# Layer 2 of the last pair of tiles split around its output projection; the last tile cut at column 288

## The chip, the cores and the metric

The kernel runs on one core of one Trainium2 chip, with the engines PE (TensorE, matrix multiply), DVE (VectorE), ACT (ScalarE), POOL (GpSimd) and SP (SyncE), which wait for each other through semaphores. The metric is device time in microseconds (us) of one execution, as the median of the runs; a lower one is better.

## The reference

One input x (2048 rows of 448 features, bf16) is normalised once, and the sum of x, a linear attention A and a dense layer B is returned:

```python
xn = _layernorm(x)
# A: 16 heads of 28
q, k, v = split(xn @ wqkv)
phi(q) = [softmax(q @ w_phi), softmax(-q @ w_phi)]      # the same for k: 56 features a head
kv = einsum("bhsf,bhsd->bhfd", phi_k, v);  z = sum_s phi_k
o  = (phi_q @ kv) / (phi_q @ z + 1e-6)
A  = o.reshape(B, S, D) @ wo
# B: 448 -> 1792 -> 448
h  = silu(xn @ w1)                                       # layer 1
out = h @ w2                                             # layer 2
return x + A + B
```

## The kernel before

The 2048 rows are 16 tiles of 128 rows; two neighbouring tiles are a pair, so tiles 14 and 15 are pair 7. For each tile a PSUM bank (128 x 448, f32) collects layer 2 of B (14 slices of 128 hidden features, `hT` times `w2_sb`) and the output projection of A (`oT_sb` times `wo_sb` and `wor_sb`). Then one addition on DVE (`out_ev`, lines 998 to 1004; the profile names its line 1000) adds x or an earlier partial sum and writes the result into `x_sb`, and a DMA stores it.

Most matmuls contract over only 64 rows. TensorE is then used as two halves, rows 0 to 63 (LOW) and rows 64 to 127 (HIGH), and `rows64` (lines 902 to 925) places matmuls of the two tiles of a pair alternately on the two halves, so that a LOW one and a HIGH one run at a time. I call such a pair of simultaneous matmuls a step. A block comes in two turns: in turn "a" the first tile has the LOW half, in turn "b" the second. When a bank changes its half, `rows64` sets `o.after` to the last block that used it, and TensorE waits on its own semaphore (s_pe) for that block's end.

The order of TensorE's work is written out by hand as the string `PLAN` (lines 361 to 368), and `strict` (line 1077) chains it; DVE, ACT, POOL and the SP queue are ordered by a list scheduler (`P.schedule`, line 228) that estimates durations. The words that matter here:

- `aG7` / `bG7`: 7 of the 14 slices of layer 2 for pair 7 on the two halves, `ffn2_pair` (line 932); `@672` gives the banks, 6 for tile 14 and 7 and 2 for tile 15.
- `aW7` / `bW7`: the output projection of pair 7, `wo_pair` (line 983): 4 steps in turn a, 3 in turn b. It needs `oT_sb`, the attention's output, transposed by a DMA on the SP queue (`oT_dma`, line 981, issued in `dma_t`, line 624). In the profile `oT_sb` is part of the tile `vaug`.
- `bW1`: the second turn of pair 1's projection, 3 steps; it belongs to other tiles.
- `E14` / `E15`: layer 2 of one tile with all 128 rows as one array, `ffn2_full` (line 940), followed by that tile's `out_ev`.

Tile 15 has two banks, so that its columns are finished in two pieces (`halves`, line 927, cut at column 224): the first piece is added and stored while TensorE computes the second. The store of a piece goes out on the ACT queue, that of the last piece on the SP queue. The last words of `PLAN` before the change are `bW6 bW7@672 bW1 aW7 E14 E15`. Tiles before pair 7 do not change.

Of the kernel before, what the change touches and what calls it, by code (L numbers as in the profile page):

```python
# [364 lines left out]
K6 K4 aq4@2 K12 aq8@4 bq4 K8 K2 s4 aq0@0 bq8 aq6@2 K14 bq0 bq6 bY1@45 K10 M aY1 aq2@2 aF26@0 s6 bq2 bY1 bF26 aG3@23 aY1  # L365
aU2@67 s8 aF15@0 bU2 s0 bF15 aF16@4 bG3 bF16 aU4@01 aq12@6 bU4 bq12 aU3@45 bG3 bU3 s2 aG3 aq10@0 aq14@6 bq10 s10 aW2@45
bq14 aG2 aU0@01 bG2 aG4@67 bU0 bW4 bG2 bW2 s12 bG4 aG2 s14 aW3 aG4 aU1@01 bW3 aW4 bU1 bG4 bG5@23 aU5@50 aG6@41 aU6@67
bU5 aG5 bG6 aU7@05 bU6 bG5 bG6 aG5 bU7 aG6 aW0@67 bW5 bW0 aW5 aW6 aW1@05 bW6 bW7@672 bW1 aW7 E14 E15"""


def bass_parallel_sum__linear_kernel_hedgehog__dense_activation_silu__prompt_kernel(
# [10 lines left out]
    S, D, H, DH, FF = 2048, 448, 16, 28, 1792  # L382
# [3 lines left out]
    FT = FF // 128  # L386
# [21 lines left out]
    with es:  # L408
        def sb(name, shape, dt):
            return es.enter_context(nc.sbuf_tensor(name, shape, dt))  # L410
# [25 lines left out]
        w2_sb = sb("w2_sb", [128, FT, D], BF16)  # L436
        hT = sb("hT", [128, FT, S], BF16)
# [54 lines left out]
        banks = [psum[:, i * 512:(i + 1) * 512] for i in range(8)]  # L492
# [10 lines left out]
        def d_mm(n):  # L503
            return max(n * 0.4167 + 2.5, 40.0)
# [10 lines left out]
        def pe_mms(mms, name, dur=None, keys_w=(), mode=128):  # L515
            def fn(e):
                r = None
                for dst, lhsT, rhs, st, sp in mms:
                    r = e.matmul(dst, lhsT, rhs, start=st, stop=sp, skip_group_check=True)  # L519
                return r  # L520
            n = 1
            for _, cnt in mms[0][2].ap[1:]:
                n *= cnt
            o = P.op("pe", dur if dur is not None else d_mm(n), fn, reads=[m[1] for m in mms] + [m[2] for m in mms],
                     writes=[m[0] for m in mms], keys_w=keys_w, name=name, mode=mode)
            o.words = 2 * len(mms)
            return o
# [20 lines left out]
        def memset(dst, v, n, name, eng="pool"):  # L548
            P.op(eng, d_pool(n, 0.5), lambda e: e.memset(dst, v), writes=[dst], name=name)
# [289 lines left out]
        def ones_column(t0, t1):  # L839
            dst = ek_pairs(t0, t1)[:, :, 0:2 * EW].rearrange("p i (h f) -> p i h f", f=DH)[:, :, :, DF]  # L840
            memset(dst, 1.0, 290 * (t1 - t0), f"one{t0}")
# [55 lines left out]
        def opens(bs):  # L897
            fresh.update(bs)
            for b in bs:
                half_of.pop(b, None)  # L900
# [25 lines left out]

        def halves(t, bs):

            cuts = (0, D) if len(bs) == 1 else (0, D // 2, D)
            return [(b, slice(0, c1 - c0), slice(c0, c1)) for b, c0, c1 in zip(bs, cuts, cuts[1:])]  # L930

        def ffn2_pair(p, turned, bs, f0, f1, last):
            both = []
            for side in range(2):
                i = side ^ turned
                both.append([(b, ds, hT[LO_HI[side], ft, (2 * p + i) * 128:(2 * p + i + 1) * 128], w2_sb[LO_HI[side], ft, cs])
                             for ft in range(f0, f1) for b, ds, cs in halves(2 * p + i, bs[i])])
            rows64(*both, "ffn2_mm", (f1 - f0) * d_mm(D), 0.0, last)

        def ffn2_full(t, bs):  # L940
            for b, ds, cs in halves(t, bs):
                pe_mms([(banks[b][:, ds], hT[:, ft, t * 128:(t + 1) * 128], w2_sb[:, ft, cs], False, ft == FT - 1) for ft in range(FT)],
                       "ffn2_mm", dur=FT * d_mm(cs.stop - cs.start))
                out_ev(t, banks[b][:, ds], x_sb[:, t, :], cs)

        def y_ev(t, b):
            fb = banks[b][:, 0:D]
            P.op("dve", d_dve(448), lambda e: e.tensor_tensor(Y_sb[:, t, :], fb, x_sb[:, t, :], ALU.add),  # L948
                 reads=[fb, x_sb[:, t, :]], writes=[Y_sb[:, t, :]], name="y_ev")
# [5 lines left out]
        def att(p, turned, bs):  # L955
            both = []
            for side in range(2):
                i = side ^ turned
                both.append([(bs[i], slice(c * 2 * DA, (c + 1) * 2 * DA), ph_slots(slot(2 * p + i))[LO_HI[side], 0, c, :],
                              KVm[LO_HI[side], c, :, :].rearrange("p j e -> p (j e)")) for c in range(CC)])  # L960
            rows64(*both, "U_mm", CC * 31.2, 400.0, turned)
            if turned:
                for i in range(2):
                    normalise(2 * p + i, banks[bs[i]])
# [33 lines left out]
        def out_ev(t, ob, addend, cs):  # L998
            res = x_sb[:, t, :]
            P.op("dve", d_dve(cs.stop - cs.start), lambda e: e.tensor_tensor(res[:, cs], ob, addend[:, cs], ALU.add),  # L1000
                 reads=[ob, addend[:, cs]], writes=[res[:, cs]], name="out_ev")
            P.dma(lambda e: e.dma_start(out=rows_of(out, t, t + 1)[:, 0, cs], in_=res[:, cs]), 100.0, lat=1200.0, reads=[res[:, cs]], name="out_dma", out_slot=ob_cnt[0] % NOS,
                  eng="sp" if cs.start else "act")
            ob_cnt[0] += 1
# [4 lines left out]
        def finish_pair(p, bs):  # L1009
            for i in range(2):  # L1010
                out_ev(2 * p + i, banks[bs[i][0]][:, 0:D], addend(2 * p + i), slice(0, D))
# [26 lines left out]
        for word in "tr0a tr0 tr1 00a 10a 01a 11a 00b 10b 01b 11b tr2 20 21 tr3 02 12 22 03 13 23".split():  # L1038
# [3 lines left out]
            f, t = int(word[0]), int(word[1])  # L1042
# [41 lines left out]
        blocks, bank_of, done = {}, {}, {}  # L1084
        open_kind = {"F": F, "v": v_block, "k": k_block, "q": q_block}

        def pair_banks(p, at):
            if at:
                b = [int(c) for c in at]
                bank_of[p] = (b[:1], b[1:])  # L1090
                opens(b)
            return bank_of[p]

        for word in PLAN.split():
            n0 = len(P.ops)
            kind, arg = word[0], word[1:]
            if kind == "r":
                b, f = (0, 2, AUX)[int(arg)], head[int(arg)]
                pe_mms(f[1](), "rest", dur=d_mm(512), mode=64)
                f[3]()  # L1100
            elif kind in "ab":
                turned = kind == "b"
                kind, (arg, _, at) = arg[0], arg[1:].partition("@")
                t = int(arg)
                if kind in open_kind:
                    if turned:
                        blocks[kind, t][2](1)
                        blocks[kind, t][3]()
                    else:
                        blocks[kind, t] = open_kind[kind](t, int(at))  # L1110
                        blocks[kind, t][2](0)
                elif kind == "U":
                    if at:
                        blocks[kind, t] = [int(c) for c in at]
                        opens(blocks[kind, t])
                    att(t, turned, blocks[kind, t])
                elif kind in "GY":
                    bs = pair_banks(t, at)
                    k = done.get((t, turned), 0)
                    done[t, turned] = k + FP  # L1120
                    done[t] = done.get(t, 0) + FP
                    ffn2_pair(t, turned, bs, k, k + FP, done[t] == 2 * FT + (0 if kind == "Y" else 2))
                    if kind == "Y" and done[t] == 2 * FT:
                        for i in range(2):
                            y_ev(2 * t + i, bs[i][0])
                else:
                    assert kind == "W"
                    done[t] = done.get(t, 0) + 1
                    wo_pair(t, turned, pair_banks(t, at), done[t] == 2 * FT + 2)
                if kind in "GW" and t < FP and done[t] == 2 * FT + 2:  # L1130
                    finish_pair(t, bank_of[t])
            elif kind == "f":
                fold_k(*map(int, arg.split("@")))
            elif kind == "g":
                fold_q(*map(int, arg.split("@")))
            elif kind == "K":
                t0 = int(arg)
                kv(range(t0, t0 + 2))
                if t0 < NEK:
                    ones_column(t0, t0 + 2)  # L1140
            elif kind == "M":
                kvm()
                for n in range(NO):
                    memset(o_sb[:, n, 0:64] if n % 2 else o_sb[:, n, D:512], 0.0, 64, "o0")
            elif kind == "s":
                scale_rows(int(arg), False)
            else:
                assert kind == "E"
                t = int(arg)
                ffn2_full(t, bank_of[t // 2][t % 2])  # L1150
            strict(n0)
        P.schedule()
        order = P.schedule(P.fetches())
# [100 lines left out]
```

## Time and profile before

| what | value |
|---|---|
| median of 3 runs | 147.05 us (146.95 to 147.09) |
| the profiled execution | 147.63 us, of which the profile's span covers 146.4 us |
| granted TensorE clock | 1.00 |
| PE busy | 141.0 us (96% of the span), 1947 matmuls |
| DVE busy | 89.5 us, ACT 79.4 us, POOL 75.1 us |
| stretch 136.17 to 138.80 us | PE busy 2.01 of 2.63 us |
| stretch 144.40 to 146.40 us | PE busy 0, DVE busy 0.34 us |

A timeline row gives start, duration from the first start to the last end, engine, line, operation, what is written and read, the shape, and the number of instructions; in brackets stands the idle time of the engine before it and what ended it. A matmul's duration in these rows includes the time to drain the array, and the next one starts before that is over: the distance from start to start is what a matmul costs in a row of them.

### The profile page before, as it was taken

To read this page: it belongs to the slowest core of one execution; us is meant where nothing else is said; L and a number is where in the kernel's file an instruction comes from. 1 tells how busy PE (TensorE), PEld (TensorE's weight loads), DVE (VectorE), ACT (ScalarE), POOL (GpSimd) and SP (SyncE) were. 2 spreads that over 40 slices of the span, in tenths; PEclk is the share of its full clock that TensorE was granted. 3 is DMA by queue.
4 is the path that set the end of the run, shared out by engine and by line. 5 is a ranking of instruction groups with operands and counts; after the bars stand their busy time and mean duration, and the time that the engine had idled before them with its cause. 6 is when DMAs were issued, how large, how long until landed. Compare 5 with 4: busy or idle time off the path is not lost.

```text
span 146.4 us, 4511 instructions
## 1 busy us (share of the span) xinstructions
PE 141.0 (96%) x1947; PEld 82.2 (56%) x1947; DVE 89.5 (61%) x195; ACT 79.4 (54%) x96; POOL 75.1 (51%) x95
## 2 busy tenths in 40 slices
PE   7789999999999999999999999999999999999894
PEld 7675445445444544476787655465555555555563
DVE  1949898610770059939049999937794394445622
ACT  4556956579996999979878948254710000000000
POOL 8808568620197008799935999991597400000000
PEclk9999999999999999999999999999999999999999
DMA  4999998755980000000000068859599899534412
GB/s 94 340 348 269 284 147 108 149 91 92 356 245 4 0 2 4 0 0 4 0 4 4 4 120 167 122 109 171 109 177 165 187 193 190 80 72 108 159 63 63
DMA packets 44500, 17.59 MB, mean 120 GB/s; under 512 B 37040, under 2 KB 44096, under 8 KB 44480
## 3 DMA queue, kind: packets, MB, share of 16 engines
q1 hardware_dynamic: 41648, 15.10, 52.5%
q10 hardware_dynamic: 2704, 2.17, 5.4%
q8 instruction: 15, 0.25, 0.7%
q14 instruction: 5, 0.04, 0.1%
q0 software_dynamic: 128, 0.03, 0.1%
HBM read 6.57 MB, written 1.84 MB: 57 GB/s over the span
## 4 chain that ended last, share of the span: by engine, by line
PE 77%; DVE 10%; DMA 7%; issue 2%; SPq 2%; ACT 1%; ACTq 0%; DVEq 0%
PE psum L519 77%; DVE Rec L836 7%; DMA phT<-in_B_w_dram 4%; DMA vaug<-vaug 3%; DVE Rec L837 2%; SPq L556 1%; SPq L624 1%; ACT Ek_sb L542 1%; DVE vaug L979 0%; DVE Y_sb L948 0%; DVE kvsum L885 0%; PE psum L536 0%; DVE x_sb L1000 0%; DVE rden L974 0%; DVE den L972 0%
## 5 line engine op out<-in xcount | busy, mean ns | idle before, releaser
L519 PE MATMUL psum<-xnT,phT 64*128 64x512 bf16 (+1 forms) x428 | 46.7, 350 | 1.3 <-DMA phT<-in_B_w_dram 1.2
L519 PE MATMUL psum<-w_sb,hT 64*128 64x448 bf16 (+2 forms) x434 | 46.1, 343 | 0.0
L836 DVE TENSOR_REDUCE Rec<-Ek_sb 128x32 f32<-128x896 bf16 (+1 forms) x20 | 24.4, 1251 | 18.8 <-ACT Ek_sb L542 18.7
L542 ACT ACTIVATE hT<-psum 128x1024 bf16<-128x1024 f32 x28 | 27.7, 1024 | 11.4 <-PE psum L519 11.2
L519 PEld LDWEIGHTS psum<-xnT,phT 64*128 64x128 bf16 (+1 forms) x428 | 22.4, 95 | 19.5 <-DMA phT<-in_B_w_dram 0.8
L519 PEld LDWEIGHTS psum<-w_sb,hT 64*128 64x128 bf16 (+1 forms) x434 | 23.0, 94 | 17.4 <-issue 0.2
L873 POOL TENSOR_TENSOR RA<-Ek_sb,Rec 128x896 bf16<-128x896 bf16 x16 | 27.1, 1723 | 5.8 <-DVE Rec L837 4.9
L519 PE MATMUL psum<-Wqk,xnT 64*128 64x432 bf16 x224 | 24.4, 342 | 0.0
L542 ACT ACTIVATE Ek_sb<-psum 128x864 bf16<-128x864 f32 x24 | 20.3, 915 | 6.3 <-PE psum L519 4.2
L846 POOL TENSOR_TENSOR Ek_sb<-Ek_sb,Rec 128x896 bf16<-128x896 bf16 x8 | 13.4, 1698 | 18.4 <-DVE Rec L837 18.4
L519 PEld LDWEIGHTS psum<-Wqk,xnT 64*128 64x128 bf16 x224 | 10.9, 94 | 8.3
L542 ACT ACT_TABLE_LOAD x11 | 14.1, 1283 | 1.0 <-PEq L1239 0.8
L846 POOL TENSOR_TENSOR phT<-phT,Rec 128x896 bf16<-128x896 bf16 x8 | 13.4, 1697 | 1.5 <-issue 0.9
L1000 DVE TENSOR_TENSOR x_sb<-psum,x_sb 128x448 bf16<-128x448 f32 (+1 forms) x13 | 7.2, 583 | 9.1 <-PE psum L519 9.1
L519 PE MATMUL psum<-wv,xnT 64*128 64x448 bf16 x112 | 12.2, 349 | 0.0
L519 PE MATMUL psum<-wo_sb,vaug 64*128 64x448 bf16 (+1 forms) x102 | 10.9, 338 | 0.6 <-DMA vaug<-vaug 0.6
L701 DVE BATCH_NORM_STATS2 st<-x_sb 128x6 f32<-128x448 bf16 x16 | 9.6, 602 | 2.9 <-DMA x_sb<-in_A_x_dram 2.9
L716 DVE TENSOR_SCALAR RA<-x_sb,mv,rstd 128x384 bf16<-128x384 bf16 (+4 forms) x29 | 9.0, 347 | 1.5 <-POOL rstd L712 1.2
L979 DVE TENSOR_TENSOR vaug<-psum,rden 128x448 bf16<-128x448 f32 x16 | 9.2, 619 | 0.0
L836 DVE TENSOR_REDUCE Rec<-phT 128x64 f32<-128x1792 bf16 x4 | 8.0, 1992 | 1.8 <-ACT phT L542 1.8
L837 DVE RECIPROCAL Rec<-Rec 128x32 f32<-128x32 f32 (+1 forms) x24 | 8.8, 395 | 0.2
L519 PEld LDWEIGHTS psum<-wv,xnT 64*128 64x128 bf16 x112 | 5.4, 94 | 5.6 <-ACT vaug L542 0.5
(60 smaller groups left out, 108.0 us busy)
## 6 DMA issues: line engine op xcount, KB each, us to landing
out_dram<-x_sb ACTq DMA_DIRECT2D x15, 112.0 KB, 2.2
w_sb<-in_B_w_dram SPq DMA_DIRECT2D x1, 1568.0 KB, 7.5
x_sb<-in_A_x_dram SPq DMA_DIRECT2D x3, 448.0 KB, 6.5
wo_sb<-in_A_wo_dram SPq DMA_DIRECT2D x2, 336.0 KB, 7.4
phT<-in_B_w_dram SPq DMA_DIRECT2D x1, 576.0 KB, 7.6
phT<-in_B_w_dram SPq DMA_DIRECT2D x2, 256.0 KB, 5.0
phT<-in_B_w_dram ACTq DMA_DIRECT2D x1, 384.0 KB, 5.2
wv<-in_A_wqkv_dram SPq DMA_DIRECT2D x1, 336.0 KB, 7.2
```

The source lines that it names most:

```text
L519: r = e.matmul(dst, lhsT, rhs, start=st, stop=sp, skip_group_check=True)
L542: P.op("act", d_act(n), lambda e: e.activation(dst, src, func, scale=scale), reads=[src], writes=[dst], table=table, name=name, **keys)
L556: P.dma(lambda e: e.dma_start(out=dst, in_=src), n / 280.0, writes=[dst], name=name, eng=eng, lat=lat)
L624: o = P.dma(lambda e: e.dma_start_transpose(out=dst, in_=src), xfer, reads=[src] if kw.pop("sbuf", True) else [], writes=[dst], name=name, ...
L701: P.op("dve", 590, lambda e: e.bn_stats(st6[:, t, :], xs), reads=[xs], writes=[st6[:, t, :]], name=f"bnst{t}", okeys_w=["ln"])
L716: P.op("dve", dur, lambda e: e.tensor_scalar(dst, x_sb[:, t, c0:c1], mv[:, t, 0:1], rstd[:, t:t + 1], ALU.subtract, ALU.mult), reads=[xs, ...
L836: P.op("dve", 50 + 967 * n, lambda e: e.tensor_reduce(R2, E4, AXL.X, ALU.add), reads=[E4], writes=[R2], name="Ssum")
L837: P.op("dve", 135 + 210 * n, lambda e: e.reciprocal(R2, R2), reads=[R2], writes=[R2], name="Rrec")
L846: P.op("pool", 1700, lambda e: e.tensor_tensor(E3, E3, Rk[:, :, None].broadcast_to([128, 32, DH]), ALU.mult), reads=[E3, Rk], writes=[E3], ...
L873: P.op("pool", 1700, lambda e: e.tensor_tensor(dst, Eq, Rq.rearrange("p (c j) -> p c j", c=CC)[:, :, :, None].broadcast_to([128, CC, 4, DH ...
L979: P.op("dve", 620, lambda e: e.tensor_tensor(o3, U3[:, :, 0:DH], rden[:, uq, :, None].broadcast_to([128, H, DH]), ALU.mult), reads=[U3[:, ...
L1000: P.op("dve", d_dve(cs.stop - cs.start), lambda e: e.tensor_tensor(res[:, cs], ob, addend[:, cs], ALU.add), reads=[ob, addend[:, cs]], wri ...
```

## The change

The plan's tail becomes `bW6 aG7@672 aW7 bW1 bG7 bW7 E14 E15`. Layer 2's slices 0 to 6 of tiles 14 and 15 are computed as 64-row steps: `aG7` stands ahead of `aW7`, `bG7` ahead of `bW7`. `E14` and `E15` compute only slices 7 to 13. Tile 15 is cut at column 288 instead of 224, so its pieces have 288 and 160 columns.

```diff
-bU5 aG5 bG6 aU7@05 bU6 bG5 bG6 aG5 bU7 aG6 aW0@67 bW5 bW0 aW5 aW6 aW1@05 bW6 bW7@672 bW1 aW7 E14 E15"""
+bU5 aG5 bG6 aU7@05 bU6 bG5 bG6 aG5 bU7 aG6 aW0@67 bW5 bW0 aW5 aW6 aW1@05 bW6 aG7@672 aW7 bW1
+bG7 bW7 E14 E15"""
...
-            cuts = (0, D) if len(bs) == 1 else (0, D // 2, D)
+            cuts = (0, D) if len(bs) == 1 else (0, 288, D)
...
-        def ffn2_full(t, bs):
+        def ffn2_full(t, bs, f0):
             for b, ds, cs in halves(t, bs):
-                pe_mms([(banks[b][:, ds], hT[:, ft, t * 128:(t + 1) * 128], w2_sb[:, ft, cs], False, ft == FT - 1) for ft in range(FT)],
-                       "ffn2_mm", dur=FT * d_mm(cs.stop - cs.start))
+                pe_mms([(banks[b][:, ds], hT[:, ft, t * 128:(t + 1) * 128], w2_sb[:, ft, cs], False, ft == FT - 1) for ft in range(f0, FT)],
+                       "ffn2_mm", dur=(FT - f0) * d_mm(cs.stop - cs.start))
                 out_ev(t, banks[b][:, ds], x_sb[:, t, :], cs)
...
-                ffn2_full(t, bank_of[t // 2][t % 2])
+                ffn2_full(t, bank_of[t // 2][t % 2], done[t // 2, False])
```

In the built programs TensorE's order is the same up to and with `bW6`; after it the change has 90 matmuls for 69. The orders of DVE, ACT, POOL and SP are the same but for the shapes of the two pieces of tile 15 and of their stores.

## The prediction

> **What bounds the kernel now.** I read the page first: PE is busy 96% of the span at a granted clock of 1.00, so what counts is where TensorE stands still and what comes after it. Then the chain that ended last, in order of time. Its end:
>
> ```profile
> 93.55 36.59 PE psum L519 x574
> ...
> 131.36 1.19 SPq L624
> ...
> 132.64 4.01 DMA vaug<-vaug
> 136.65 0.14 issue
> 136.79 7.53 PE psum L519 x62
> 144.32 0.02 issue
> 144.34 0.39 DVE x_sb L1000
> ```
>
> TensorE carries the chain from 93.55 us. Near the end the chain leaves it once: the last transposing DMA of the attention's output lands at 136.65 us, 4.01 us after its issue, and TensorE's last 62 matmuls start 0.14 us later. Then the timeline of that stretch:
>
> ```profile
> 135.44 0.73 PE L519 MATMUL psum<-wo_sb,vaug 64*128 64x448 bf16 x6
> 136.21 1.16 DVE L1000 TENSOR_TENSOR x_sb<-psum,x_sb 128x448 bf16<-128x448 f32 x2 [0.62 <-PE psum L519]
> 136.79 1.89 PE L519 MATMUL psum<-wo_sb,vaug 64*128 64x224 bf16 x24 [0.62 <-DMA vaug<-vaug]
> 138.49 0.37 PE L519 MATMUL psum<-wor_sb,vaug 64*128 64x448 bf16 x3
> 138.80 5.50 PE L519 MATMUL psum<-w_sb,hT 128*128 128x448 bf16 x42
> 141.66 0.62 DVE L1000 TENSOR_TENSOR x_sb<-psum,x_sb 128x448 bf16<-128x448 f32 x1 [2.37 <-PE psum L519]
> 143.00 0.39 DVE L1000 TENSOR_TENSOR x_sb<-psum,x_sb 128x224 bf16<-128x224 f32 x1 [0.72 <-PE psum L519]
> 144.34 0.39 DVE L1000 TENSOR_TENSOR x_sb<-psum,x_sb 128x224 bf16<-128x224 f32 x1 [0.95 <-PE psum L519]
> 144.83 0.36 SPq L1002 DMA_DIRECT2D out_dram<-x_sb  x1
> ```
>
> bW7 is first in line at 136.79 and waits for that DMA; E14 and E15 (x42), which wait for nothing, stand behind it. After the last matmul come an addition of 224 columns, a store on SP, and its landing: 1.57 us from the store's start at 144.83 to the span's end at 146.40.
>
> **Prices.** The same view gives them, from earlier stretches:
>
> ```profile
> 111.48 2.81 PE L519 MATMUL psum<-w_sb,hT 64*128 64x448 bf16 x28
> 114.13 0.73 PE L519 MATMUL psum<-wo_sb,vaug 64*128 64x448 bf16 x6
> ...
> 122.20 0.62 PE L519 MATMUL psum<-KVm,phT 64*128 64x58 bf16 x32
> 122.66 2.81 PE L519 MATMUL psum<-w_sb,hT 64*128 64x448 bf16 x28
> ```
>
> The first 28 matmuls are 14 steps, and from their start to the next group's it is 2.65 us: 189.3 ns a step of 448 columns. A 224-column matmul costs (144.34 - 143.00)/14 = 95.7 ns by the additions that follow each piece. The line through both is 2.1 ns + 0.418 ns a column: 122.4 ns at 288 columns, 69.0 at 160. A split side of a step thus takes 122.4 + 69.0 = 191.4 ns, as 2 x 95.7 did. Additions on DVE average 618 ns at 448 columns and 392 at 224, so 1.01 ns a column: 457 ns at 288, 327 at 160.
>
> **The change, part by part.**
>
> *The gap.* bW6's three steps start at 135.44, 135.63 and 135.82; the next could start at 136.01. It starts at 136.79, so the gap is 0.78 us from start to start (the row's 0.62 leaves out the drain). Now aG7 stands there. It reads `hT` and `w2_sb`, both long in place, and waits only for its banks: DVE's additions of pair 0 and of tile 10 were over by 135.03 (two in a row from 134.45 to 135.60), 0.98 us early. So the gap goes: -0.78 us. aG7 lasts 7 x 0.191 = 1.34 us, and aW7, which needs the DMA, comes at 137.35, 0.56 us after the moment at which bW7 could start before. That slack is what covers the wait; if the DMA lands later than that, the excess comes back one for one.
>
> *Moved layer 2.* Added: 14 split steps, 14 x 191.4 = 2.68 us. Removed: 7 matmuls of 448 in E14 (1.325 us) and half of E15, 28 x 95.7 - 7 x (122.4 + 69.0) = 1.34 us. Net +0.015 us. Layer 2 is neither cheaper nor dearer; it is only movable in this form. W7 keeps its 7 steps, now split 288/160.
>
> *The added wait.* bG7 turns the banks over and waits (s_pe) for aW7. Between them stands bW1, 3 steps = 0.57 us; behind the wait stand bW7, E14 and E15, and everything after. Before, aW7 waited for bW7 with the same bW1 between, and its fourth step starts at 138.49, just 9 steps after 136.79 (1.70 us): that wait cost nothing. I take 0. Without the cover it would be about a drain, 350 - 189 = 160 ns, and a signal; the range holds it.
>
> *64 to 128 rows.* Before, ten steps from 136.79 end at 138.70 and E14 starts at 138.80: 0.10 us. There is still one such passage: 0.
>
> *The narrow end.* The last piece has 160 columns: 392 - 327 = 65 ns less on DVE, -0.065 us. It must not find DVE busy: E15's first piece is ready 0.483 us (7 x 69.0) before the second, and its addition takes 0.457. That is a slack of 0.03, so I take 0, and at worst a tenth.
>
> *The stores.* The two stores of tile 15 start 0.42 us apart instead of 1.41 (143.42 and 144.83). That of 288 columns (72 KB) on ACT starts near 143.58 and lands 1.6 to 1.7 later by the rows of 56 and 112 KB, at 145.25; the last, on SP, starts near 144.00 and lands at 145.5 at the row's 1.5. It stays the last by 0.25. It is 40 KB instead of 56, in as many rows, and may share engines with the other for a moment: from -0.05 to +0.2, I take 0, since the landing is mostly not transfer (56 KB kept the engines busy some 0.35 of 1.6 us).
>
> *More instructions.* 21 matmuls with their weight loads are 42 more on PE. The instruction queue's row has 15 fetches for 2 x 1947 = 3894, one for 260; the last falls at 134 to 135 us, with about 170 instructions to go. 212 to go is still under 260: no sixteenth.
>
> **The sum.** -0.78 + 0.015 - 0.065 = -0.83 us. In times: aG7 136.01, aW7 137.35, bW1 138.12, bG7 138.68, bW7 140.02, E14 140.70, E15 142.02, its second piece 142.88 to 143.36; the addition starts 0.21 after that as before (144.13 to 144.34), 143.57 to 143.90; store at 144.00, end of the span 145.57. The profiled execution goes from 147.63 to 146.80. Its 1.23 us outside the span don't change. The median of the runs lies 0.58 under the profiled one; with the same difference, 147.05 - 0.83 = 146.22 us.
>
> **A rule against it.** The narrowest matmuls in rows are 12 of 128 columns with all 128 rows, from 9.03 to the next group's start at 9.70: 56 ns each, though a 128 x 128 weight load is listed with 98 ns. On the halves, 16 steps of 58 columns (the third row above) go from 122.20 to 122.66, 29 ns each, with loads listed at 94. So loads overlap far beyond what 160 columns need. The Trainium skill ("TensorE: Matmul & The Clock Gate", section "Back-to-back issue gap") speaks of a sustained 81 ns per matmul at N=128 for alternating weight loads and matmuls, because both set the spacing. By that figure a 160-column matmul would take at least 81 ns instead of 69, an estimate of 28 x 12 ns = 0.34 us more, and the time 146.56. These rows disagree with it.
>
> **The rivals.**
>
> 1. *The gap is not there, or shorter, without the profiler.* The last transpose landed 4.01 us after its issue, its nine neighbours from 2.4 to 4.6 with a median of 3.5. Landing 3.23 us after its issue or earlier, it would not have held TensorE at all; then only 0.05 is gained: 147.0. For it: the timed runs are 0.58 us shorter than the profiled one, and no view says where. If all of it lay here, the gap would be 0.20 and the time 146.8. Against: the median landing of 3.5 still leaves a gap of 0.27, and in those 0.58 us there is also what surrounds the span.
>
> 2. *A floor for narrow matmuls.* If a weight load's listed 94 to 98 ns were the least distance, each of 28 matmuls of 160 columns would take about 26 ns more, 0.73 in all: 146.95. This is the mechanism of the page's rule above. For it: 224 columns (95.7 ns) just hide such a load, 160 don't. Against: the 56 and 29 ns of the rows.
>
> 3. *Slower: weight loads left bare.* If the load for the 160-column matmul could not start until the 288-column one of the same half is through, 21 split steps and 7 matmuls of E15 would each grow by a whole load: 28 x 94 ns = 2.63 us, net +1.8, or 148.85. It decides from 30 ns a matmul on (0.83/28). For it: a split of 288/160 was never run here, and two matmuls on one half with one tile's weights in succession are just where a second buffer is needed. Against: the same pattern at 224/224 in bW7 and aW7 ran at 189 ns a step.
>
> That the change doesn't do what it says I exclude: in the built order aG7 stands between bW6 and aW7.
>
> **How the numbers follow.** The sum holds: 0.64, from 146.05 to 146.45. Rival 1: 0.15, of which 0.07 with a shorter gap (under 146.76) and 0.08 with next to none. Rival 2: 0.10, of which 0.06 with a mild floor (under 146.76) and 0.04 with the whole of it. Rival 3: 0.11. A measurement of this kernel tells about 0.2% from no change, 0.29 us, so faster means under 146.76: 0.64 + 0.07 + 0.06 = 0.77, the same 0.08 + 0.04 = 0.12, slower 0.11. The range goes down to 145.9, for a transpose that lands as late as 4.6, which aG7 would cover as well, and up to 147.0 for the cases without a gain; the slower case is left out.
>
> **What would show it.** Right: no idle time of PE with "DMA vaug<-vaug" in the tail; matmuls of w_sb,hT with 64 rows starting at 136.0; the wo_sb group at 137.35; the 128-row group at 140.7 with 21 matmuls; the last addition at 143.57 with about 0.33 us. Wrong: PE waiting for the same DMA at aW7; a distance of aG7 to aW7 well over 1.34 us (a floor, or bare loads); idle time before bG7 (the turned banks); or a last store that lands more than 1.6 us after its issue.

## The result and the profile after

| | before | after |
|---|---|---|
| median of 22 runs each, on the same chips | 147.07 us (146.02 to 148.24) | 146.24 us (145.75 to 146.95) |
| ratio, 95% interval | | 0.9948 (0.9932 to 0.9964) |
| profiled execution, its span | 147.63, 146.4 us | 146.72, 145.5 us |
| PE busy, matmuls | 141.0 us, 1947 | 141.3 us, 1968 |

The kernel is 0.83 us faster by the medians, where 0.83 was forecast (146.22); the interval allows 0.53 to 1.00. The chain that ended last no longer leaves TensorE for the transposing DMA (start, duration, what carries it):

```profile
93.53 49.97 PE psum L520 x707
143.53 0.33 DVE x_sb L1001
```

One run of 707 matmuls goes from 93.53 us to the end. Before, there were 574 up to 130 us, then DVE, the SP queue and the DMA, and 62 more. The tail in the timeline (lines are one higher than before, since `PLAN` has one more):

```profile
135.42 0.73 PE L520 MATMUL psum<-wo_sb,vaug 64*128 64x448 bf16 x6
...
135.99 1.50 PE L520 MATMUL psum<-w_sb,hT 64*128 64x448 bf16 x21
...
137.31 0.76 PE L520 MATMUL psum<-wo_sb,vaug 64*128 64x448 bf16 x9
...
138.63 1.51 PE L520 MATMUL psum<-w_sb,hT 64*128 64x288 bf16 x21
...
139.98 0.74 PE L520 MATMUL psum<-wo_sb,vaug 64*128 64x288 bf16 x9
...
140.65 2.84 PE L520 MATMUL psum<-w_sb,hT 128*128 128x448 bf16 x21
142.18 0.62 DVE L1001 TENSOR_TENSOR x_sb<-psum,x_sb 128x448 bf16<-128x448 f32 x1 [2.17 <-PE psum L520]
143.04 0.81 DVE L1001 TENSOR_TENSOR x_sb<-psum,x_sb 128x288 bf16<-128x288 f32 x2 [0.23 <-PE psum L520]
143.94 0.35 SPq L1003 DMA_DIRECT2D out_dram<-x_sb  x1
```

No PE row carries a bracket. aG7 starts 0.57 us (three steps) after bW6's first matmul, where bW7 before started 1.35 us after it. The two last additions are one merged row: 0.81 us for 288 and 160 columns, the second 0.33 of it by the chain.

The runs of one kernel scatter by up to about 1 us to either side, more than the change. The profiles show one place for it. In the kernel before and in the seven experiments that left the start alone, the load that the chain begins with took 5.0 to 5.8 us, and TensorE's first uninterrupted stretch (345 matmuls) started at 9.44 to 10.26 us. (In the changed kernel the chain begins with another load and doesn't show that stretch.) So I compare tails: from the start of bW6's six matmuls to the end of the last addition. That is 144.73 - 135.44 = 9.29 us before and 143.86 - 135.42 = 8.44 after: -0.85. From the start of the 345 matmuls to bW6 it was 125.35 to 125.42 us in every kernel whose chain shows that stretch.

### The profile page after: what moved, and what is told of

The parts are those of the page before. It is cut to its first block, busy times and chain, and to the rows that moved or that the text cites. A ratio compares the mean times of both kernels' runs of the same rounds, so it can differ in the third digit from the quotient of the medians.

```text
span 145.5 us, 4553 instructions
## 1 busy us (share of the span) xinstructions
PE 141.3 (97%) x1968; PEld 83.0 (57%) x1968; DVE 89.5 (62%) x195; ACT 79.5 (55%) x96; POOL 75.2 (52%) x95
## 4 chain that ended last, share of the span: by engine, by line
PE 68%; DVE 18%; POOL 5%; DMA 4%; issue 3%; ACT 1%; DVEq 0%; POOLq 0%; ACTq 0%
PE psum L520 68%; DVE Rec L837 7%; DMA Wp<-in_A_w_phi_dram 4%; DVE RA L717 4%; DVE st L702 3%; DVE Rec L838 2%; POOL rstd L713 1%; POOL Wp L557 1%; DVE mv L703 1%; POOL vaug L550 1%; DVE Wqk L695 1%; ACT Ek_sb L543 1%; POOL ve L711 1%; POOL BD L632 0%; DVE Y_sb L949 0%
## 5 line engine op out<-in xcount | busy, mean ns | idle before, releaser
L520 PE MATMUL psum<-w_sb,hT 64*128 64x448 bf16 (+4 forms) x455 | 46.5, 341 | 0.0
L520 PEld LDWEIGHTS psum<-w_sb,hT 64*128 64x128 bf16 (+1 forms) x455 | 23.6, 94 | 17.2 <-issue 0.2
L1001 DVE TENSOR_TENSOR x_sb<-psum,x_sb 128x448 bf16<-128x448 f32 (+2 forms) x13 | 7.2, 583 | 7.5 <-PE psum L520 7.4
L520 PE MATMUL psum<-wo_sb,vaug 64*128 64x448 bf16 (+2 forms) x102 | 11.3, 338 | 0.0
```

## The experiments

In every edit below the changed kernel is the base unless the text says otherwise. Ratios are to the kernel before, run on the same chip.

### Only the cut undone

```diff
-            cuts = (0, D) if len(bs) == 1 else (0, 288, D)
+            cuts = (0, D) if len(bs) == 1 else (0, D // 2, D)
```

> The changed kernel with tile 15 cut at 224 again, so only the narrow end is undone. My theory: TensorE is as in the changed kernel up to the start of tile 15's first piece (near 142.0 us), the pieces take 7 x 95.7 = 0.67 us each, the last addition takes 0.39 us instead of 0.33, and it is ready at the same time, so the span ends 0.06 to 0.07 us later than the changed kernel's 145.5, near 145.55. Rival (narrow matmuls cost a floor, or the two stores of the pieces disturb each other): this one ends earlier than the changed kernel.

Ratio 0.9942 (0.9913 to 0.9970). The span, 144.9, is shorter than the changed kernel's, but only because this execution started 0.6 us earlier. Its tail:

```profile
134.79 0.73 PE L520 MATMUL psum<-wo_sb,vaug 64*128 64x448 bf16 x6
...
142.90 0.39 DVE L1001 TENSOR_TENSOR x_sb<-psum,x_sb 128x224 bf16<-128x224 f32 x1 [0.28 <-PE psum L520]
```

142.90 + 0.39 - 134.79 = 8.50 us, 0.06 longer than with the cut at 288. The sum had 0.065. The expected span of 145.55 missed since it left out that the start moves.

### Only the cut

```diff
-            cuts = (0, D) if len(bs) == 1 else (0, D // 2, D)      # base: the kernel before
+            cuts = (0, D) if len(bs) == 1 else (0, 288, D)
```

> The kernel before with the cut at 288 and nothing else. My theory: the wait for the transposing DMA stays (0.62 us listed as idle at bW7, 0.78 from start to start); the second piece has 14 x 69.0 = 0.97 us on TensorE, the last addition 0.33 us: the end 0.06 us earlier than before, span near 146.3, time within 0.1 of before. Rival (the whole gain comes from the narrow end): 0.8 us faster than before, 146.2.

Ratio 0.9992 (0.9965 to 1.0018): no gain that the runs can tell. The profile has a wait longer than expected:

```profile
134.91 0.73 PE L519 MATMUL psum<-wo_sb,vaug 64*128 64x448 bf16 x6
135.69 1.16 DVE L1000 TENSOR_TENSOR x_sb<-psum,x_sb 128x448 bf16<-128x448 f32 x2 [0.62 <-PE psum L519]
136.84 1.89 PE L519 MATMUL psum<-wo_sb,vaug 64*128 64x288 bf16 x24 [1.20 <-DVE x_sb L1000]
```

The bracket names DVE, and that is to be read with care. bW7 needs DVE only for its banks, which were free after the additions before these (the first of a pair from 133.92), and the addition that it names ends 0.01 after bW7 starts. The last transpose was issued at 132.11 and took 4.6 us: it landed at 136.71, 0.13 before bW7. So the wait was again the DMA's, 136.84 - 135.48 = 1.36 us from start to start. From bW7 on it is 7.88 us to the last addition's end (144.72), against 7.94 before: the cut is worth 0.06. The whole tail, 144.72 - 134.91 = 9.81 us, is 0.52 longer than before, because this transpose took 4.6 us instead of 4.0; the span is the same 146.4 only because this execution started earlier.

### The same matmuls, the cover taken away

```diff
-... bW6 aG7@672 aW7 bW1
+... bW6 aW7@672 aG7 bW1
 bG7 bW7 E14 E15"""
```

> The changed kernel with aG7 moved from ahead of aW7 to behind it: the same matmuls in the same form, but the first work after bW6 needs the transposed output again. My theory: TensorE waits 0.6 to 0.8 us at aW7 for the DMA and everything behind it is later by that: span near 146.3, time near 147.0, the same as before within 0.1. Rival (the 64-row form or less work in E14 and E15 is what gains): still 0.8 faster than before, 146.2.

Ratio 0.9984 (0.9957 to 1.0011), median 147.19 against 147.26.

```profile
135.62 0.73 PE L520 MATMUL psum<-wo_sb,vaug 64*128 64x448 bf16 x6
...
136.96 0.75 PE L520 MATMUL psum<-wo_sb,vaug 64*128 64x448 bf16 x9 [0.61 <-DMA vaug<-vaug]
...
144.03 0.81 DVE L1001 TENSOR_TENSOR x_sb<-psum,x_sb 128x288 bf16<-128x288 f32 x2 [0.23 <-PE psum L520]
```

The DMA's wait is back, 136.96 - 136.19 = 0.77 us, and the tail is 144.84 - 135.62 = 9.22 us: 0.78 over the changed kernel's. All matmuls, their forms and the cut are the changed kernel's; only aG7 stands elsewhere. The place is the gain, and the medians of the timed runs show it too.

### The turn of the banks without its cover

The plan's tail, put on one line:

```diff
-bW6 aG7@672 aW7 bW1 bG7 bW7 E14 E15"""
+bW6 aG7@672 aW7 bG7 bW7 bW1 E14 E15"""
```

> The changed kernel with bW1 moved behind bW7, so that bG7 follows aW7 at once and its wait for aW7's end has no cover. My theory: TensorE stands still there for the drain of a matmul (0.16 us) and a signal, 0.2 to 0.3 us from start to start, and the end is later by that: span 145.7 to 145.8, time near 146.5. Rival (the wait costs nothing, cover or no cover): span 145.5.

Ratio 0.9955 (0.9930 to 0.9980), median 146.67.

```profile
137.47 0.38 PE L520 MATMUL psum<-wor_sb,vaug 64*128 64x448 bf16 x3
137.91 1.51 PE L520 MATMUL psum<-w_sb,hT 64*128 64x288 bf16 x21
...
142.90 0.81 DVE L1001 TENSOR_TENSOR x_sb<-psum,x_sb 128x288 bf16<-128x288 f32 x2 [0.23 <-PE psum L520]
```

aW7's last step starts at 137.47 and bG7 at 137.91 instead of 0.19 later, so a bare turn costs 0.25 us. No bracket shows it, because the rows count the drain as busy: aW7's last one lasts until 137.85. The tail is 143.71 - 135.02 = 8.69 us, 0.25 over the changed kernel. bW1 between the two turns is what made the added wait free.

### Three slices ahead instead of seven

```diff
-                    done[t, turned] = k + FP
-                    done[t] = done.get(t, 0) + FP
+                    n = 3 if t == 7 else FP
+                    done[t, turned] = k + n
+                    done[t] = done.get(t, 0) + n
...
-                    ffn2_pair(t, turned, bs, k, k + FP, ...)
+                    ffn2_pair(t, turned, bs, k, k + n, ...)
```

> The changed kernel with only slices 0 to 2 of layer 2 moved (aG7 and bG7 of 3 slices, E14 and E15 of 11). Cover ahead of aW7 is 3 x 0.191 = 0.57 us instead of 1.34. My theory: the rest of the wait shows. The last transposes of the runs so far let TensorE go on 0.78 to 1.37 us after bW6's steps, so 0.2 us is left where the DMA lands as in the kernel before, more where the run is early; start of bW6's six matmuls to the end of the last addition 8.65 us against 8.44 of the changed kernel and 9.29 of the one before; time near 146.5. Rival (what gains is the amount of layer 2 in the 64-row form): three sevenths of the gain, 146.85, with no idle time at aW7.

Ratio 0.9991 (0.9961 to 1.0021): the times tell it neither from no change nor from -0.4 us. The profile does:

```profile
134.88 0.73 PE L520 MATMUL psum<-wo_sb,vaug 64*128 64x448 bf16 x6
135.45 0.74 PE L520 MATMUL psum<-w_sb,hT 64*128 64x448 bf16 x9
...
136.48 0.75 PE L520 MATMUL psum<-wo_sb,vaug 64*128 64x448 bf16 x9 [0.29 <-DMA vaug<-vaug]
...
143.46 0.32 DVE L1001 TENSOR_TENSOR x_sb<-psum,x_sb 128x160 bf16<-128x160 f32 x1 [0.30 <-PE psum L520]
```

aG7 ends its three steps at 136.02 and aW7 starts at 136.48: 0.46 us are left of the wait, more than the 0.2 expected, since the transpose took 4.3 us here. The tail is 8.90 us, 0.46 over the changed kernel's 8.44 and 0.39 under the 9.29 before. The rival's three sevenths of the gain would be 0.36, so the size of the gain doesn't tell the two apart. The idle time at aW7 does, which the rival excludes, and so does the run with aG7 behind aW7, where the same seven slices moved as in the change and the profile shows a gain of 0.07 only. So the gain follows the length of the cover up to the wait, and not the amount of layer 2 that is moved.

### A last piece of 64 columns

```diff
-            cuts = (0, D) if len(bs) == 1 else (0, 288, D)
+            cuts = (0, D) if len(bs) == 1 else (0, 384, D)
```

> The changed kernel with tile 15 cut at 384, so its last piece has 64 columns. My theory (a weight load hides behind any matmul from 58 columns on): the steps stay at 191 ns (162.6 + 28.8), aG7 lasts 1.34 us, the second piece's seven matmuls take 7 x 29 = 0.20 us; but the first piece's addition (0.55 us) is still under way, so the last addition starts late and the tail from bW6's start to the last addition's end is 8.7 us against 8.44. Rival (a floor of 81 to 98 ns a narrow matmul): steps of 0.24 to 0.26 us, aG7 1.7 to 1.8 us, the second piece 0.57 to 0.69 us.

There is one execution of this kernel, 146.91 us, so only its profile counts.

```profile
135.89 1.50 PE L520 MATMUL psum<-w_sb,hT 64*128 64x448 bf16 x21
...
137.21 0.76 PE L520 MATMUL psum<-wo_sb,vaug 64*128 64x448 bf16 x9
...
140.55 2.84 PE L520 MATMUL psum<-w_sb,hT 128*128 128x448 bf16 x21
142.09 0.62 DVE L1001 TENSOR_TENSOR x_sb<-psum,x_sb 128x448 bf16<-128x448 f32 x1 [2.17 <-PE psum L520]
143.22 0.69 DVE L1001 TENSOR_TENSOR x_sb<-psum,x_sb 128x384 bf16<-128x384 f32 x2 [0.51 <-PE psum L520]
```

A narrower window of the same timeline has the last seven matmuls in a row of their own:

```profile
143.02 0.37 PE L520 MATMUL psum<-w_sb,hT 128*128 128x64 bf16 x7
```

aG7 lasts 137.21 - 135.89 = 1.32 us: seven steps of 189 ns with a matmul of 64 columns in each. In the 128-row form one matmul of 64 columns is listed with 193 ns and all seven with 0.37 us, so they started about 29 ns apart, and E14 and E15 together take the same 2.84 us as with 288/160; had each of the seven cost its weight load of 98 ns, it would have been 3.3. Now the first piece is so late that the last addition queues behind it, and the tail is 143.91 - 135.32 = 8.59 us, 0.15 over the changed kernel (0.26 expected; most of the difference is that the two additions in a row took 0.69 us, where the prediction's price by columns gives 0.78).

### Another cover: the second turn of pair 1

```diff
-... bW6 bW7@672 bW1 aW7 E14 E15"""      # base: the kernel before
+... bW6 bW1 bW7@672 aW7 E14 E15"""
```

> The kernel before with bW1 moved from behind bW7 to ahead of it; layer 2 and the cut are as before. bW1's 3 steps (0.57 us) stand where TensorE waited, but aW7 now follows bW7 at once. My theory (any work that needs nothing new covers the wait): the wait shrinks by 0.57 to about 0.2, and the bare turn of the banks costs the 0.25 us that the run with bW1 behind bW7 showed, so the tail from bW6's start to the last addition's end is 9.29 - 0.57 + 0.25 = 8.97 us and the time about 146.9. Rival (only the moved layer 2 helps): 147.2.

Ratio 0.9998 (0.9965 to 1.0031), medians 146.97 and 147.14. The chain:

```profile
135.76 0.63 DVE x_sb L1000
136.39 0.77 PE psum L519 x7
137.16 0.05 issue
137.20 6.39 PE psum L519 x50
```

bW1 ends its steps at 136.12 and bW7 starts at 136.39: 0.27 us are left. (The chain names DVE again; the transpose landed at 132.18 + 4.1 = 136.28.) The bare turn before aW7 costs 0.24. The tail is 144.01 - 134.98 = 9.03 us (8.97 expected), 0.26 better than before by the profile, and too little for the timed runs. Other work covers the wait as well, but this one takes the cover away from the turn.

### Why the transpose is late: the instruction transfer

In each run so far the last transpose took 4.0 to 4.6 us, the one ahead of it 2.4, and one transfer of TensorE's instruction queue (q8) fell within it. If its place goes by the number of instructions ahead of it, fewer of them at the start move it. Base: the kernel before.

```diff
-        for i in range(38):
+        for i in range(24):
             o = P.op("pe", 107.0, lambda e: e.matmul(banks[3][:, 0:128], ones_bf[:], ones_bf[:], ...
```

> The kernel before with 24 instead of 38 idle warm-up matmuls at the start (they compute nothing that is used), so TensorE's stream is 28 instructions shorter ahead of the tail. The instruction queue's last transfer, which in each run fell within the last transpose (134 to 135 us), comes about 14 matmuls, 1.3 us, later. Theory A (that transfer is why the last transpose takes 4.0 to 4.6 us and not 2.4): it lands up to 1.6 us earlier, TensorE's wait at bW7 shrinks by 0.5 us or goes, time 146.3 to 146.6. Theory B (the transpose is late for other reasons, such as the stores that begin at 134): it takes 4.0 again, wait and time as before, 147.2. In both the start may be some tenths slower, if the clock is granted later.

The q8 transfer came after 137 us, the transpose took 2.4 us, and bW7 did not wait: the tail is 144.74 - 136.23 = 8.51 us. But the start paid for it, and the ratio is 1.0029 (0.9992 to 1.0066):

```profile
6.42 2.74 PE psum L519 x24
9.16 0.43 PE psum L536 x4
```

Four 128-column matmuls took 0.43 us, 108 ns each, where the kernel before needed 0.22, and the 345 matmuls started at 10.81 instead of 10.09. The granted clock is listed at 1.00 all the same. The Trainium skill ("TensorE: Matmul & The Clock Gate", Part 1) says that the array starts at half its clock and is released by some 4 us of activity, with 107 and 56 ns per matmul of 128 columns; the two durations here agree. So I kept the length of the warm-up and took only the instructions:

```diff
-        for i in range(38):
-            o = P.op("pe", 107.0, lambda e: e.matmul(banks[3][:, 0:128], ones_bf[:], ones_bf[:], ...
+        for i in range(24):
+            c = 4 if i < 5 else 1
+            o = P.op("pe", 107.0 * c, lambda e, c=c: e.matmul(banks[3][:, 0:128 * c], ones_bf[:], ones_bf[:, None, :].broadcast_to([128, c, 128]), ...
```

> The kernel before with its warm-up of the same length in fewer instructions (5 matmuls of 512 columns and 19 of 128 instead of 38 of 128; they compute nothing that is used). TensorE's stream is 28 instructions shorter, its clock should be granted as early as before. Layer 2, the plan and the cut are as before. Theory A (the instruction transfer within the last transpose made it late): the last transpose lands 2.4 us after its issue, TensorE doesn't wait at bW7, tail from bW6's start to the last addition's end 8.51 us instead of 9.29, time 0.7 to 0.8 us under before, as fast as the changed kernel within 0.1. Theory B (only the late, cold start of the run with 24 warm-up matmuls changed the transpose): 4.0 us, 9.29, no gain.

Ratio 0.9949 (0.9927 to 0.9971), medians 146.53 and 147.34: as much as the change, with the old plan. The last transpose by the DMA issues (the last figure is the time to landing), and the q8 transfer by the DMA queues, in the kernel before, where it stands in the window 134 to 135 us:

```profile
vaug<-vaug SPq DMA_TRANSPOSE x1, 4.0
q8 instruction: 1, 0.02, 5.5%
```

Here it stands in the window 135 to 136 us:

```profile
vaug<-vaug SPq DMA_TRANSPOSE x1, 2.5
q8 instruction: 1, 0.02, 9.5%
```

The transpose lands at 134.5, ahead of the q8 transfer, which starts at 135.8. TensorE goes straight through:

```profile
134.94 2.44 PE L519 MATMUL psum<-wo_sb,vaug 64*128 64x448 bf16 x30
...
143.05 0.39 DVE L1001 TENSOR_TENSOR x_sb<-psum,x_sb 128x224 bf16<-128x224 f32 x1 [0.95 <-PE psum L519]
```

Tail: 143.44 - 134.94 = 8.50 us. The same warm-up in the changed kernel:

> The changed kernel with the same shorter warm-up. Theory A: the last transpose lands 2.4 us after its issue here too, but TensorE had not waited for it any more, so nothing is gained beyond the changed kernel: tail 8.44 us, time within 0.15 of the changed kernel (0.8 under before). Rival (an earlier landing shortens the tail further, or the transfer now falls where it costs something else): more than 0.3 us from the changed kernel, either way.

Ratio 0.9950 (0.9919 to 0.9982), tail 143.83 - 135.39 = 8.44 us, the transpose 2.5 us. The cover and the shorter stream are two remedies for one wait and don't add. No run here beats the changed kernel by more than the scatter.

With the q8 transfer inside, the last transpose took 4.0 to 4.6 us in nine kernels; with it after, 2.4 to 2.5 in three. In those three the scheduler also moved one earlier transpose (`phT<-RA`, issued at 110.95 us in the kernel before) behind two others, so they don't differ in the transfer alone. But the same two lengths stand side by side within each kernel. In the kernel before, the last six transposes of `vaug` took 4.2, 3.5, 2.5, 2.5, 2.4 and 4.0 us; q8 transfers started at 126.0 us, within the first two, and at 134.6, within the last. In the run with fewer instructions the six took 2.4, 4.2, 3.0, 2.5, 2.4 and 2.5, and the transfer at 126.7 fell within the second and the third. Over all twelve kernels, none of these transposes (of one the trace has no landing) without a q8 transfer took more than 2.5 us. How the transfer holds a transpose up stays open.

## Why the prediction was right, point by point

| step of the sum | predicted | measured |
|---|---|---|
| the gap covered | -0.78 | -0.78 (bW6 to its successor 1.35, now 0.57); -0.78 again by moving aG7 alone |
| layer 2 in another form | +0.015 | aG7 1.32 and bG7 1.35 us, 2.67 against 2.68 predicted |
| the added wait, covered by bW1 | 0 | 0; 0.25 when bare (0.2 was the guess) |
| the last piece of 160 columns | -0.065 | -0.06, twice |
| its addition behind the first's | 0, slack 0.03 | 0: it follows TensorE, not the first addition, and ends at 143.86 (143.90 predicted) |
| last store to the span's end | 1.57, unchanged | 145.5 - 143.94 = 1.56 |
| sixteenth instruction transfer | none | 15 |
| sum | -0.83 | tail -0.85, medians -0.83 |

The mechanism is the one that was forecast, term by term, and the tail shows it to 0.02 us. That the medians agree as closely is luck, since their interval is half a microsecond wide. The step from the profiled execution to the median, 0.58 in the sum, was 0.48 in the changed kernel, and the profiled execution came out at 146.72 where 146.80 was forecast; the two misses nearly cancel.

*Rival 1* (no gap without the profiler) fell: with the wait put back the timed runs were where the kernel before is, 147.19 against 147.26. The 0.58 us between its profiled execution and its median were no sign of it: the changed kernel, which doesn't wait, has 146.72 against 146.24. Both profiled executions reached bW6 late, at 135.44 and 135.42 us, where the seven experiments that left the start alone reached it at 134.79 to 135.62; that the differences lie there is likely, but not shown.

*Rival 2* (a floor) and *rival 3* (bare loads) fell with aG7's 1.32 us and with the run at 64 columns, at 189 ns a step and some 29 ns a narrow matmul. The 81 ns of the Trainium skill ("TensorE: Matmul & The Clock Gate", section "Back-to-back issue gap") do not hold in this kernel's rows.

One thing the prediction had not seen, though its size did no harm: it took the transpose's 4.01 us as a draw from 2.4 to 4.6. For the most part it was no draw: with an instruction transfer inside, the last transpose took 4.0 to 4.6 us in each of nine kernels, without one 2.4 to 2.5, and only the rest is scatter. Its low case, a transpose of 4.6 that the cover would also hide, did occur in the run with only the cut changed, where the wait was 1.36 us; aG7's 1.32 to 1.34 is just about that long.

## What to carry to other kernels

Where an engine waits in line for a transfer, look at what stands behind the wait and needs nothing new; if it can be put ahead in a form that costs the same, the gain is the wait itself, and the cover should be as long as the longest landing that was seen. An added wait is free only with work between, so check that the cover of one wait is not taken from another. Before covering a late transfer, see what shares its time: here 14 matmuls fewer at the kernel's start were worth as much as the new order at its end.

## What the runs showed of the hardware

- One transfer of TensorE's instructions within the last transposing DMA went with 1.5 to 2.2 us of delay (4.0 to 4.6 us in nine kernels against 2.4 to 2.5 in three).
- When matmuls on one half of the array followed at once on a bank that the other half had used, the s_pe wait cost 0.24 to 0.25 us from start to start, and the idle column showed none of it.
- Matmuls of 64 columns went at about 29 ns in the 128-row form, with weight loads listed at 98 ns.
- The clock is listed as granted in full while 128-column matmuls at the start took 108 ns instead of 55.
